# A filter's transform taken about time 0, with tables of its own

## The chip, the cores and the metric

The kernel runs on one core of one Trainium2 chip. The metric is the device time of one execution in microseconds; runs are compared with runs of the same state (fast), on the same chip and in the same rounds. One execution of each kernel is profiled; all times "at" some point are from the start of that profile's span. The engines are PE (matmul), PEld (its weight loads), DVE (vector), ACT (scalar), POOL (GpSimd) and SP. Tiles named ps_... lie in PSUM, which the matmuls here write to; the other tiles lie in SBUF. To evict is to copy a result out of PSUM; a gather is a load whose rows are picked by a tile of indices.

## The reference, cut to what matters

Linear attention with a normalised output, then a long convolution in the frequency domain between two gates, for a batch of 8, 576 time steps and 512 channels:

```python
kv = np.einsum('bhsd,bhse->bhde', k, v)                    # per head, 64 x 64
out = np.einsum('bhsd,bhde->bhse', q, kv)
x = out / sqrt(mean(out * out) + 1e-6) * g_norm            # -> [8, 576, 512]
x1, x2, x3 = split(x @ w_proj, 3)
H = np.fft.rfft(filter_fft, n=576, axis=0)                 # the filter: once for all batches
x2_conv = np.fft.irfft(np.fft.rfft(x2, axis=1) * H, axis=1)
return (x1 * x2_conv * x3) @ w_out
```

The transforms are matmuls with tables of cosines and sines. The change concerns `H`, which is computed once, in the start of the kernel, and is needed before batch 0 can be multiplied by it.

## The kernel before

The start, in the order of the program: loads of the first q, k and v, of three parts of `w_proj` (wp), of the filter (fa and its mirror image fc), of batch 1 and of `w_out`, all issued by POOL; attention of batch 0; transposed tables (FW, FX); then for batch 0 the projection x2, the sums and differences of the filter (ff), the gates (ps_x), the transform of the filter (`gen_h`, tiles ps_h), attention of batch 1 (qT, kvblk), and the first product of a transformed x2 with the filter (tile tpw). From there on DVE is full until about 60 us, and then PE to the end.

The base tables are symmetric about the time 287.5, so the filter was folded about that time too: row n with row 575 - n.

```python
for a, r0, n, base in ((0, 0, 64, 0), (0, 64, 64, 1), (1, 0, 64, 2), (1, 64, 64, SB), (2, 0, 32, SB + 1)):
    nc.gpsimd.iota(fidx[r0:r0 + n, a:a + 1], ..., base=S - 1 - base, channel_multiplier=-3)
for r0, n, a, na, base, step in (...):                     # fa: three direct loads of 64, 64 and 32 rows
    nc.gpsimd.dma_start(out=fa[r0:r0 + n, a:a + na], in_=...)
for a in range(3):                                         # fc: gathers of 128, 128 and 32 rows
    n = P if a < 2 else 32
    nc.gpsimd.indirect_dma_start(out=fc[:n, a], in_=moe_filter_fft, in_offset=...fidx[:n, a:a + 1]...)
# ... cut
def fold_filter():                                         # ff = fa + fc and fa - fc, on DVE, four pieces
    ...
def gen_h(g):                                              # g = 0, 1, 2
    ...                                                    # 6 (or 12) matmuls of FW with ff into hp
    for i, (o_, ri, c1, c2) in enumerate(todo):            # a rotation by the phase of 287.5
        nc.scalar.activation(out=u[:n, i], in_=hp[:n, ri], func=AF.Copy, scale=c1)
        nc.vector.scalar_tensor_tensor(out=o_, in0=hp[:n, 1 - ri], scalar=c2, in1=u[:n, i], ...)
    if g < 2:
        nc.scalar.activation(out=HH[:n, g, 2], in_=HH[:n, g, 0], func=AF.Copy, scale=-1.0)
```

P is 128, S 576, SB 192, N1 97, DM 512 (a row of the filter is 2 KB).

## Time and profile before

| | kernel before |
|---|---|
| time, median | 242.26 us (3 runs, 242.19 to 243.76) |
| span of the profiled run | 238.0 us |
| granted PE clock, mean | 0.993 |
| first filter product (tpw) | 44.56 us |
| from there to the end of the span | 193.4 us |

The span is the profiled core's from its first to its last instruction. The last row is the one to keep: if a change touches only the start, a kernel's span should be its own first tpw plus some 193 us. Two lines of the page of before, in 40 slices of 5.95 us, are for later comparison: the granted clock of PE in tenths, and the busy share of the 16 DMA engines.

```profile
PEclk9999999999999999999999999999999999999997
DMA  6999999999099129914992399250033003400346
```

The clock is at its full value up to the last slice, and the transfers are dense for the first ten slices.

### The profile page before, as it was taken

What the parts mean: (1) busy time and instruction counts of PE and PEld (TensorE: products, weight loads), DVE (VectorE), ACT (ScalarE), POOL (GpSimd) and SP (SyncE); (2) the same over time, 40 slices, a digit from 0 to 9 for tenths busy, and PEclk for the clock granted to TensorE, in tenths of its full rate; (3) what the DMA queues carried; (4) which work ended last, traced back from release to release, by engine and by line L of the source; (5) the groups of instructions that cost most, each with busy time, mean ns of one, the idle gap of its engine ahead of it and who ended that gap; (6) DMA issues with size and microseconds to landing.
All of it is one profiled execution on the core that took longest, in us unless ns stands there. A gap on an engine that the chain in (4) does not pass through costs nothing.

```text
span 238.0 us, 4900 instructions
## 1 busy us (share of the span) xinstructions
PE 213.9 (90%) x1960; PEld 128.5 (54%) x1960; DVE 197.2 (83%) x376; ACT 156.0 (66%) x237; POOL 72.1 (30%) x96
## 2 busy tenths in 40 slices
PE   4978897685999999999999999999999999999960
PEld 1434354363576657665667566656675666566420
DVE  7759574799989798979797989797979897999860
ACT  2754528971887689776977697769776977642520
POOL 7963971490280029000910091002100210021010
PEclk9999999999999999999999999999999999999997
DMA  6999999999099129914992399250033003400346
GB/s 63 163 190 230 227 192 197 191 192 108 3 155 198 45 77 158 203 38 126 121 193 74 91 118 188 83 135 0 4 88 88 3 0 91 132 0 3 94 122 181
DMA packets 45559, 27.17 MB, mean 114 GB/s; under 512 B 22274, under 2 KB 40706, under 8 KB 45538
## 3 DMA queue, kind: packets, MB, share of 16 engines
q0 software_dynamic: 40256, 17.70, 58.8%
q1 hardware_dynamic: 5122, 8.92, 13.9%
q8 instruction: 15, 0.25, 0.4%
q10 hardware_dynamic: 160, 0.26, 0.4%
q14 instruction: 6, 0.05, 0.1%
HBM read 33.69 MB, written 9.44 MB: 181 GB/s over the span
## 4 chain that ended last, share of the span: by engine, by line
PE 61%; ACT 15%; DVE 8%; DMA 8%; issue 3%; POOL 3%; POOLq 0%; DVEq 0%; ACTq 0%
PE ps_x L428 20%; PE ps_out L488 10%; ACT qT L256 6%; PE ps_x L378 6%; DMA fc<-in_moe_filter_fft_dram,fidx 5%; DMA km<-in_k_dram 3%; PE ps_x L384 2%; PE ps_x L369 2%; PE ps_o L265 2%; PE ps_r L280 2%; ACT kvblk L234 2%; PE ps_invo L454 2%; PE ps_inve L454 2%; PE ps_kv L223 2%; ACT osb L271 2%
## 5 line engine op out<-in xcount | busy, mean ns | idle before, releaser
L428 PE MATMUL ps_x<-x,wp 128*128 128x288 bf16 x512 | 68.0, 286 | 1.5 <-DVE FX L210 1.5
L428 PEld LDWEIGHTS <-wp 128*128 128x128 bf16 x512 | 49.8, 98 | 15.3 <-issue 2.6
L411 POOL TENSOR_TENSOR Y<-tpw 128x1024 bf16<-128x1024 f32 (+1 forms) x9 | 21.2, 2354 | 68.7 <-PE ps_x L428 43.2
L434 DVE TENSOR_TENSOR g<-ps_x,x 128x576 bf16<-128x576 f32 x32 | 24.1, 754 | 9.8 <-ACT x L432 9.7
L432 ACT CAST x<-ps_x 128x576 bf16<-128x576 f32 x32 | 20.7, 646 | 10.4 <-PE ps_x L428 10.4
L70 POOL DMA_DIRECT2D km<-in_k_dram x9 | 7.8, 871 | 64.4 <-PE ps_kv L223 64.4
L488 PE MATMUL ps_out<-wo,yg 128*128 128x512 bf16 x112 | 26.6, 379 | 0.0
L281 ACT ACTIVATE rstd<-ps_r,bias_eps 128x576 bf16<-128x576 f32 x32 | 23.3, 742 | 4.8 <-PE ps_r L280 4.8
L496 ACT COPY ot<-ps_out 128x1024 f32<-128x1024 f32 (+1 forms) x17 | 15.9, 937 | 13.8 <-PE ps_out L488 13.8
L266 ACT ACTIVATE sq<-ps_o 128x576 bf16<-128x576 f32 x32 | 20.7, 653 | 5.6 <-PE ps_o L265 5.6
L408 DVE TENSOR_TENSOR tpw<-ps_X,HH 128x1024 f32<-128x1024 f32 (+1 forms) x16 | 19.5, 1221 | 5.1 <-PE ps_X L406 4.4
L271 ACT ACTIVATE osb<-ps_o,g_col 128x576 bf16<-128x576 f32 x28 | 20.8, 742 | 0.0
L409 DVE TENSOR_TENSOR tpw<-ps_X,HH 128x1024 f32<-128x1024 f32 (+1 forms) x16 | 19.4, 1213 | 0.0
L458 ACT COPY os<-ps_invo 128x576 f32<-128x576 f32 x14 | 9.0, 640 | 12.9 <-PE ps_x L372 5.1
L488 PEld LDWEIGHTS <-yg 128*128 128x128 bf16 x112 | 10.8, 98 | 10.4
L265 PE MATMUL ps_o<-qT,kvblk 128*128 128x288 bf16 x64 | 12.8, 287 | 3.7 <-ACT kvblk L234 2.1
L378 PE MATMUL ps_x<-wp,ab 128*128 128x512 bf16 x64 | 15.5, 381 | 0.6 <-DVE ab L307 0.3
L256 ACT COPY qT<-ps_qT 128x1152 bf16<-128x1152 bf16 x14 | 15.1, 1122 | 0.1
L280 PE MATMUL ps_r<-sq,ind 128*128 128x288 bf16 x64 | 13.1, 286 | 1.6 <-ACT osb L271 0.8
L79 POOL DMA_DIRECT2D qb<-in_q_dram x16 | 12.5, 784 | 6.3 <-DMA wp<-in_moe_w_proj_dram 3.1
L535 PE MATMUL ps_w<-kvblk,ind 128*128 128x512 bf16 x33 | 11.1, 486 | 3.7 <-DVE ind L103 3.4
L374 ACT CAST x<-ps_x 128x1024 bf16<-128x1024 f32 x8 | 8.1, 1016 | 8.4 <-PE ps_x L372 8.4
(177 smaller groups left out, 414.8 us busy)
## 6 DMA issues: line engine op xcount, KB each, us to landing
out_dram<-ot SPq DMA_DIRECT2D x28, 256.0 KB, 3.3
qb<-in_q_dram POOLq DMA_DIRECT2D x16, 288.0 KB, 7.1
km<-in_k_dram POOLq DMA_DIRECT2D x7, 512.0 KB, 6.2
vm<-in_v_dram POOLq DMA_DIRECT2D x7, 512.0 KB, 8.4
wp<-in_moe_w_proj_dram POOLq DMA_DIRECT2D x3, 512.0 KB, 10.6
out_dram<-ot SPq DMA_DIRECT2D x10, 128.0 KB, 3.2
km<-in_k_dram POOLq DMA_DIRECT2D x2, 256.0 KB, 5.6
kt<-in_k_dram POOLq DMA_DIRECT2D x8, 64.0 KB, 5.7
```

What stands on the lines that cost most here:

```text
L256: nc.scalar.copy(out=o_, in_=i_)
L266: nc.scalar.activation(out=s['sq'][:, j].rearrange("p (a b) -> p a b", a=2), in_=op[:, :, 0:TH], func=AF.Square)
L271: nc.scalar.activation(out=o_, in_=op[:, :, 0:TH], func=AF.Copy, scale=g_col)
L281: nc.scalar.activation(out=s['rstd'][:, j].rearrange("p (a b) -> p a b", a=2), in_=r2[:, :, 0:TH], func=AF.Abs_reciprocal_sqrt, scale=1.0 ...
L378: nc.tensor.matmul(pp[:, h], ab[:, j, h * SB:h * SB + P], wp[:, j, DM:2 * DM], start=(j == 0), stop=(j == NDC - 1))
L408: nc.vector.tensor_mul(out=t_[:n, 0], in0=xp[:n], in1=HH[:n, g, 1:3])
L409: nc.vector.tensor_mul(out=t_[:n, 1], in0=xp[:n], in1=HH[:n, g, 0:2])
L411: nc.gpsimd.tensor_add(out=Y[:n, 2 * g:2 * g + 2], in0=t_[:n, :, 0], in1=t_[:n, :, 1])
L428: nc.tensor.matmul(pp[:, h, 0:TH], w_, x[:, j, h * TH:(h + 1) * TH], start=(j == 0), stop=(j == NDC - 1))
L432: nc.scalar.copy(out=x1, in_=pp[:, :, 0:TH])
L434: nc.vector.tensor_mul(out=st[b]['g13'][:, dc].rearrange("p (a b) -> p a b", a=2), in0=pp[:, :, 0:TH], in1=x1)
L488: nc.tensor.matmul(pp[:, cc], yg[:, dc, c * P:(c + 1) * P], wo[:, dc], start=(dc == 0), stop=(dc == NDC - 1))
```

## The change

The intent: a filter folded about time 0 (row t with row 576 - t) has a transform that needs no rotation by a phase, so each group of outputs is evicted by one scaled copy instead of ACT and DVE products in turn. It needs tables of its own (FH), which are computed on ACT in an idle gap of 5 us; the base tables shrink from 288 to 192 columns. The filter is now held as 97 partitions of three consecutive rows each. The core of the diff:

```diff
@@ the loads @@
-    for a, r0, n, base in ((0, 0, 64, 0), (0, 64, 64, 1), (1, 0, 64, 2), (1, 64, 64, SB), (2, 0, 32, SB + 1)):
-        nc.gpsimd.iota(fidx[r0:r0 + n, a:a + 1], pattern=[[0, 1]], base=S - 1 - base, channel_multiplier=-3)
-    for r0, n, a, na, base, step in ((0, 64, 0, 2, 0, 2), (64, 64, 0, 2, 1, SB - 1), (0, 32, 2, 1, SB + 1, 1)):
-        nc.gpsimd.dma_start(out=fa[r0:r0 + n, a:a + na], in_=bass.AP( ... ap=[[3 * DM, n], [step * DM, na], [1, DM]]))
+    nc.gpsimd.iota(fidx, pattern=[[-1, 3]], base=S, channel_multiplier=-3)
+    nc.gpsimd.memset(fidx[0:1, 0:1], 0)
+    nc.gpsimd.dma_start(out=fa[:N1], in_=bass.AP( ... ap=[[3 * DM, N1], [1, 3 * DM]]))
     for a in range(3):
-        n = P if a < 2 else 32
-        nc.gpsimd.indirect_dma_start(out=fc[:n, a], out_offset=None, in_=moe_filter_fft,
-                                     in_offset=bass.IndirectOffsetOnAxis(ap=fidx[:n, a:a + 1], axis=0))
+        nc.gpsimd.indirect_dma_start(out=fc[:N1, a], out_offset=None, in_=moe_filter_fft,
+                                     in_offset=bass.IndirectOffsetOnAxis(ap=fidx[:N1, a:a + 1], axis=0))
@@ new tables @@
+    def filter_angles():                    # DVE: 3 products of 289 columns, 3 passes over 97x867
+    def filter_tables():
+        preload_act_table_set("trig_and_small")
+        keep(nc.scalar.activation(out=a_, in_=r_, func=AF.Abs))
+        keep(nc.scalar.activation(out=FH[:N1, :, 1], in_=r_, func=AF.Sin, scale=2 * W0))
+        keep(nc.scalar.activation(out=FH[:N1, :, 0], in_=a_, func=AF.Sin, scale=-2 * W0, bias=cosb[:N1, 0:1]))
+        rsqrt_set()
@@ fold_filter @@
-            for r, c in ((slice(0, P), slice(0, 2)), (slice(0, 32), slice(2, 3))):
-                tc.keep_in_program_order(op(out=ff[r, i, c], in0=fa[r, c], in1=fc[r, c]))
+            tc.keep_in_program_order(op(out=ff[:N1, i], in0=fa[:N1], in1=fc[:N1]))
@@ gen_h @@
-        for i, (o_, ri, c1, c2) in enumerate(todo):
-            nc.scalar.activation(out=u[:n, i], in_=hp[:n, ri], func=AF.Copy, scale=c1)
-            nc.vector.scalar_tensor_tensor(out=o_, in0=hp[:n, 1 - ri], scalar=c2, in1=u[:n, i], op0=ALU.mult, op1=ALU.add)
-        if g < 2:
-            nc.scalar.activation(out=HH[:n, g, 2], in_=HH[:n, g, 0], func=AF.Copy, scale=-1.0)
+        if g == 2:
+            nc.scalar.activation(out=HM, in_=hp, func=AF.Copy, scale=2.0 / S)
+            return
+        nc.scalar.activation(out=HH[:n, g, 0:2], in_=hp[:n], func=AF.Copy, scale=asc[:n] if g == 0 else 2.0 / S)
+        nc.vector.tensor_scalar_mul(out=HH[:n, g, 2], in0=HH[:n, g, 0], scalar1=-1.0)
```

Cut: the smaller `tables()`, the index and angle tiles, and the order of `qtr(1)` and `gen_h(2)`, which change places.

More of the change, by code (lines that the diff above doesn't have):

```diff
@@ L116 @@
     nc.gpsimd.iota(ki[64:128, 2:3], pattern=[[0, 1]], base=2 + 3 * 32, channel_multiplier=3)
-    tvi = work.tile([P, 2 * SB], I32, name="tvi", tag="yg", bufs=3)
-    nc.gpsimd.iota(tvi, pattern=[[2 * SB, 2], [2, 3], [6, 64]], base=1, channel_multiplier=0)
+    tvi = work.tile([P, SB], I32, name="tvi", tag="yg", bufs=3)
+    nc.gpsimd.iota(tvi, pattern=[[2, 3], [6, 64]], base=1, channel_multiplier=0)
+    NF = N1 + SB
+    kri = work.tile([P, NF], I32, name="kri", tag="yg", bufs=3)
+    nc.gpsimd.iota(kri[:, 0:N1], pattern=[[3, N1]], base=0, channel_multiplier=0)
+    nc.gpsimd.iota(kri[:, N1:NF], pattern=[[1, 2], [3, SB // 2]], base=1, channel_multiplier=0)
+    tci = consts.tile([P, 3], I32)
+    nc.gpsimd.iota(tci, pattern=[[1, 3]], base=0, channel_multiplier=3)
     ident = consts.tile([P, P], BF16)
@@ L138 @@
     fidx = consts.tile([P, 3], I32)
-    for a, r0, n, base in ((0, 0, 64, 0), (0, 64, 64, 1), (1, 0, 64, 2), (1, 64, 64, SB), (2, 0, 32, SB + 1)):
-        nc.gpsimd.iota(fidx[r0:r0 + n, a:a + 1], pattern=[[0, 1]], base=S - 1 - base, channel_multiplier=-3)
-    for r0, n, a, na, base, step in ((0, 64, 0, 2, 0, 2), (64, 64, 0, 2, 1, SB - 1), (0, 32, 2, 1, SB + 1, 1)):
-        nc.gpsimd.dma_start(out=fa[r0:r0 + n, a:a + na], in_=bass.AP(
-            tensor=moe_filter_fft.tensor, offset=moe_filter_fft.offset + base * DM,
-            ap=[[3 * DM, n], [step * DM, na], [1, DM]]))
+    nc.gpsimd.iota(fidx, pattern=[[-1, 3]], base=S, channel_multiplier=-3)
+    nc.gpsimd.memset(fidx[0:1, 0:1], 0)
+    nc.gpsimd.dma_start(out=fa[:N1], in_=bass.AP(
+        tensor=moe_filter_fft.tensor, offset=moe_filter_fft.offset, ap=[[3 * DM, N1], [1, 3 * DM]]))
     for a in range(3):
-        n = P if a < 2 else 32
-        nc.gpsimd.indirect_dma_start(out=fc[:n, a], out_offset=None, in_=moe_filter_fft,
-                                     in_offset=bass.IndirectOffsetOnAxis(ap=fidx[:n, a:a + 1], axis=0))
+        nc.gpsimd.indirect_dma_start(out=fc[:N1, a], out_offset=None, in_=moe_filter_fft,
+                                     in_offset=bass.IndirectOffsetOnAxis(ap=fidx[:N1, a:a + 1], axis=0))
     load_q(1)
@@ L155 @@
     nc.vector.tensor_copy(out=kcol, in_=ki)
-    tv = work.tile([P, TH], FP32, name="tv", tag="yg", bufs=3)
-    nc.vector.tensor_copy(out=tv, in_=tvi[:, 0:TH])
-    IV = consts.tile([P, 6, TH], BF16)
-    asc = consts.tile([P, 3], FP32)
-    cf = consts.tile([P, 3, 3], FP32)
-    ph = consts.tile([P, 2, 3], FP32)
-    nc.scalar.activation(out=ph[:, 0], in_=kcol, func=AF.Sin, scale=-W0, bias=cosb[:, 0:1])
-    nc.scalar.activation(out=ph[:, 1], in_=kcol, func=AF.Sin, scale=W0)
+    tv = work.tile([P, SB], FP32, name="tv", tag="ot", bufs=3)
+    nc.vector.tensor_copy(out=tv, in_=tvi)
+    IV = consts.tile([P, 6, SB], BF16)
+    asc = consts.tile([P, 1], FP32)
+    nc.vector.memset(asc, 2.0 / S)
+    nc.vector.memset(asc[0:1], 1.0 / S)
+    nc.vector.memset(asc[96:97], 1.0 / S)
     for c, tag in enumerate(("x", "Y", "g13")):
-        ang = work.tile([P, 2, TH], FP32, name="ang", tag=tag, bufs=1 if c else 2)
+        ang = work.tile([P, 2, SB], FP32, name="ang", tag=tag, bufs=1 if c else 2)
         a_, r_ = ang[:, 0], ang[:, 1]
@@ L176 @@
         nc.scalar.activation(out=IV[:, 2 * c], in_=a_, func=AF.Sin, scale=cosb[:, 2 + h:3 + h], bias=cosb[:, h:h + 1])
-    tc.keep_in_program_order(nc.scalar.preload_act_table_set("abs_reciprocal_sqrt_and_small"))
+    rsqrt_set = lambda: tc.keep_in_program_order(nc.scalar.preload_act_table_set("abs_reciprocal_sqrt_and_small"))
+    rsqrt_set()
+    FH = consts.tile([P, 3, 2, NF], BF16)
+    kr = consts.tile([P, NF], FP32)
+    tcol = consts.tile([P, 3], FP32)
+    fang = {}
+    def filter_angles():
+        nc.vector.tensor_copy(out=kr, in_=kri)
+        nc.vector.tensor_copy(out=tcol, in_=tci)
+        a_, r_ = (work.tile([P, 3, NF], FP32, name="fang", tag="ot", bufs=3)[:N1] for _ in range(2))
+        for a in range(3):
+            nc.vector.tensor_scalar_mul(out=a_[:, a], in0=kr[:N1], scalar1=tcol[:N1, a:a + 1])
+        nc.vector.tensor_scalar(out=r_, in0=a_, scalar1=1.0 / S, scalar2=MAGIC, op0=ALU.mult, op1=ALU.add)
+        nc.vector.tensor_scalar(out=r_, in0=r_, scalar1=MAGIC, scalar2=-1.0 * S, op0=ALU.subtract, op1=ALU.mult)
+        nc.vector.tensor_tensor(out=r_, in0=r_, in1=a_, op=ALU.add)
+        fang['ar'] = a_, r_
+    def filter_tables():
+        a_, r_ = fang['ar']
+        tc.keep_in_program_order(nc.scalar.preload_act_table_set("trig_and_small"))
+        keep = tc.keep_in_program_order
+        keep(nc.scalar.activation(out=a_, in_=r_, func=AF.Abs))
+        keep(nc.scalar.activation(out=FH[:N1, :, 1], in_=r_, func=AF.Sin, scale=2 * W0))
+        keep(nc.scalar.activation(out=FH[:N1, :, 0], in_=a_, func=AF.Sin, scale=-2 * W0, bias=cosb[:N1, 0:1]))
+        rsqrt_set()
+        for p in (0, 96):
+            nc.vector.tensor_scalar_mul(out=FH[p:p + 1, 0, 0], in0=FH[p:p + 1, 0, 0], scalar1=0.5)
     g_col = consts.tile([P, 1], FP32)
@@ L181 @@
         tensor=g_norm.tensor, offset=g_norm.offset, ap=[[0, 2], [1, D]]))
-    FW = consts.tile([P, 3, 6, P], BF16)
+    FW = consts.tile([P, 2, 6, P], BF16)
     FX = consts.tile([P, 4, P], BF16)
@@ L188, in tables @@
         nc.vector.memset(FX[0:96, 0], 0.0)
-        fts = [psp.tile([P, 2, 8, P], BF16, name="ps_ft", tag="ps") for _ in range(2)]
+        d0, d1 = (psp.tile([P, 2, 8, P], BF16, name="ps_ft", tag="ps")[:, 0] for _ in range(2))
         lo, hi = slice(0, 64), slice(64, P)
-        tr = nc.tensor.transpose
-        for a in range(3):
-            n = P if a < 2 else 32
-            ts = slice(a * P, a * P + n)
-            d = fts[a // 2][:n, a % 2]
-            for i in range(6):
-                tr(d[:, i], IV[:, i, ts], ident)
-            if a == 0:
-                tr(d[96:P, 6], IV[:, 1, 0:32], ident)
-                for i in (lo, hi):
-                    tr(d[i, 7], IV[:, 1, 32:96], ident)
-            if a == 1:
-                for i in (3, 5):
-                    tr(d[hi, 6 + i // 5], IV[:, i, P:SB], ident)
-            nc.vector.tensor_copy(out=FW[:n, a], in_=d[:, 0:6])
-            if a == 0:
-                nc.vector.tensor_copy(out=FX[96:P, 0], in_=d[96:P, 6])
-                nc.vector.tensor_copy(out=FX[:, 1], in_=d[:, 7])
-            if a == 1:
-                nc.vector.tensor_copy(out=FX[hi, 2:4], in_=d[hi, 6:8])
+        tr, cp = nc.tensor.transpose, nc.vector.tensor_copy
+        for i in range(2, 6):
+            tr(d0[:, i], IV[:, i, 0:P], ident)
+        tr(d0[0:96, 0], IV[:, 0, 0:96], ident)
+        tr(d0[96:P, 6], IV[:, 1, 0:32], ident)
+        for r in (lo, hi):
+            tr(d0[r, 7], IV[:, 1, 32:96], ident)
+        for i in range(2, 6):
+            tr(d1[lo, i], IV[:, i, P:SB], ident)
+        for i in (3, 5):
+            tr(d1[hi, 6 + i // 5], IV[:, i, P:SB], ident)
+        cp(out=FW[:, 0, 2:6], in_=d0[:, 2:6])
+        cp(out=FW[lo, 1, 2:6], in_=d1[lo, 2:6])
+        cp(out=FX[hi, 2:4], in_=d1[hi, 6:8])
+        cp(out=FW[0:96, 0, 0], in_=d0[0:96, 0])
+        cp(out=FX[96:P, 0], in_=d0[96:P, 6])
+        cp(out=FX[:, 1], in_=d0[:, 7])
     x_t, st = {}, {}
@@ L317, in fold_filter @@
         for i, op in enumerate((nc.vector.tensor_add, nc.vector.tensor_sub)):
-            for r, c in ((slice(0, P), slice(0, 2)), (slice(0, 32), slice(2, 3))):
-                tc.keep_in_program_order(op(out=ff[r, i, c], in0=fa[r, c], in1=fc[r, c]))
-        nc.vector.memset(asc, 2.0 / S)
-        nc.vector.memset(asc[0:1, 0:1], 1.0 / S)
-        nc.vector.memset(asc[96:97, 0:1], 1.0 / S)
-        for i in range(2):
-            nc.vector.tensor_mul(out=cf[:, i], in0=ph[:, i], in1=asc)
-        nc.vector.tensor_scalar_mul(out=cf[:, 2], in0=cf[:, 1], scalar1=-1.0)
-        pc = hst['pc'] = consts.tile([P, 4], FP32, name="pc")
-        for r, o in ((slice(0, 64), (0, 1, 2, 0)), (slice(64, P), (2, 0, 0, 1))):
-            for i in range(4):
-                nc.gpsimd.tensor_copy(out=pc[r, i:i + 1], in_=cf[r, o[i], 2:3])
+            tc.keep_in_program_order(op(out=ff[:N1, i], in0=fa[:N1], in1=fc[:N1]))
     def gen_h(g):
@@ L336, in gen_h @@
         n = N1 if g == 0 else P
-        for ri in range(2):
+        f0 = (0, N1, N1 + P)[g]
+        for i in range(2):
             for a in range(3):
-                m = P if a < 2 else 32
+                m = N1 if a == 0 else N1 - 1
                 kw = dict(start=(a == 0), stop=(a == 2))
                 if g < 2:
-                    nc.tensor.matmul(hp[:n, ri], FW[:m, a, 2 * g + ri, 0:n], ff[:m, ri, a], **kw)
+                    nc.tensor.matmul(hp[:n, i], FH[:m, a, 1 - i, f0:f0 + n], ff[:m, 1 - i, a], **kw)
                 else:
-                    for dup in range(2):
-                        nc.tensor.matmul(hp[dup * NM:(dup + 1) * NM, ri], FW[:m, a, 4 + ri, ri * NM:(ri + 1) * NM], ff[:m, ri, a], **kw)
-        u = work.tile([P, 2, DM], FP32, name="hu", tag="ot", bufs=3)
-        if g < 2:
-            todo = [(HH[:n, g, 1], 0, cf[:n, 0, g:g + 1], cf[:n, 1, g:g + 1]),
-                    (HH[:n, g, 0], 1, cf[:n, 0, g:g + 1], cf[:n, 2, g:g + 1])]
-        else:
-            pc = hst['pc']
-            todo = [(HM[:, i], 0, pc[:, 2 * i:2 * i + 1], pc[:, 2 * i + 1:2 * i + 2]) for i in range(2)]
-        for i, (o_, ri, c1, c2) in enumerate(todo):
-            nc.scalar.activation(out=u[:n, i], in_=hp[:n, ri], func=AF.Copy, scale=c1)
-            nc.vector.scalar_tensor_tensor(out=o_, in0=hp[:n, 1 - ri], scalar=c2, in1=u[:n, i], op0=ALU.mult, op1=ALU.add)
-        if g < 2:
-            nc.scalar.activation(out=HH[:n, g, 2], in_=HH[:n, g, 0], func=AF.Copy, scale=-1.0)
+                    for h in range(2):
+                        cs = (h + i) % 2
+                        nc.tensor.matmul(hp[h * NM:(h + 1) * NM, i], FH[:m, a, cs, f0:f0 + NM], ff[:m, cs, a], **kw)
+        if g == 2:
[3 more added lines that the diff above has]
+        nc.vector.tensor_scalar_mul(out=HH[:n, g, 2], in0=HH[:n, g, 0], scalar1=-1.0)
     def proj2(b):
@@ L539 @@
     qtr(0)
+    filter_angles()
     warm(9)
@@ L550 @@
         fold(0, jj)
+    filter_tables()
     tables()
@@ L562 @@
             gen_h(0)
+            gen_h(2)
             qtr(1)
-            gen_h(2)
             kv(1)
```

## The prediction

> **What bounds the kernel now.** I first read the busy time by stretch, to see where an engine is full, then the chain of work that ended last, then the instructions in order of time for the start, because the change touches only the start (the tables, the filter and its transform; the work on batches 1 to 7 is unchanged, and so are its instructions). Columns of the first view: busy us and count of each engine, clock, DMA share, GB/s.
>
> ```profile
> core 0: us, PE busy (x) PEld busy (x) DVE busy (x) ACT busy (x) POOL busy (x), PEclk, DMA share, GB/s
> 20.00:28.00 8.00, 7.43 (x55) 3.49 (x55) 5.08 (x14) 2.78 (x5) 4.54 (x7) 1.00 1.21 241
> 28.00:36.00 8.00, 6.49 (x40) 3.52 (x38) 6.38 (x9) 2.40 (x4) 6.05 (x15) 1.00 1.57 192
> 36.00:44.50 8.50, 5.86 (x99) 2.92 (x97) 3.83 (x6) 7.49 (x13) 3.20 (x4) 1.00 1.49 195
> 44.50:60.00 15.50, 11.00 (x83) 6.93 (x83) 15.48 (x26) 8.51 (x15) 6.80 (x5) 1.00 1.30 153
> 60.00:84.00 24.00, 23.70 (x232) 15.30 (x233) 21.64 (x39) 18.47 (x28) 6.95 (x7) 1.00 0.76 105
> ```
>
> From 60 us on PE is full, and from 44.5 to 60 DVE is (15.48 of 15.5 us). Before 44.5 nothing is full but the transfers: that stretch is made of waits, and a gain has to come from it. The chain there:
>
> ```profile
> 7.84 6.48 DMA km<-in_k_dram
> 14.36 0.84 issue
> 15.20 0.49 POOL fc L147
> 15.69 0.86 issue
> 16.55 11.37 DMA fc<-in_moe_filter_fft_dram,fidx
> 28.17 1.02 issue
> 29.19 0.55 DVE FW L205
> 29.75 0.31 DVE FX L210
> 30.10 3.10 PE ps_x L428 x24
> 33.20 3.43 PE ps_h L342 x12
> 36.66 1.26 ACT hu L355 x2
> 37.92 1.01 ACT qT L256
> ...
> 42.26 0.76 DVE HM L356
> 43.10 0.70 ACT hu L355
> 43.95 0.61 issue
> 44.56 1.21 DVE tpw L408
> ```
>
> The gathered mirror of the filter (fc) is awaited until about 28. DVE takes its instructions in order, so the copies of the FW and FX tables, which need no fc, wait behind the sum ff; PE waits for their PSUM buffer; then comes the transform (ps_h), and its eviction as an ACT product followed by a DVE product, six times, ping-pong. The first filter product (tpw, 44.56) starts the DVE-bound stage, and whatever moves that instruction should move the end by as much. The start of the wait, in order of time:
>
> ```profile
> 26.02 1.01 ACT L374 CAST x<-ps_x 128x1024 bf16<-128x1024 f32 x1 [5.22 <-PE ps_x L372]
> 28.05 1.23 DVE L319 TENSOR_TENSOR ff<-fa,fc 128x1024 bf16<-128x1024 f32 x1 [2.82 <-DMA fc<-in_moe_filter_fft_dram,fidx]
> ```
>
> ACT is idle for 5.22 us before 26.02: the new tables will be computed in just that gap.
>
> **What the Trainium skill says.** "ScalarE: Activation LUTs", What ACT_TABLE_LOAD costs: a load is about 1283 ns and a switch of sets about 2.66 us with its drain; an activation costs 186 ns plus 0.833 ns an element, a pointer operand 93 ns more. The trace agrees on the load (1283 ns, twice) and on activations (427 ns at 288 columns, 612 with two pointers); in neither case did work stand ready behind the load, so it does not show the drain. "DMA: Bandwidth & Descriptors", Why a DMA increments its semaphore by 16 and not by 1: the largest k up to 16 that divides the slowest dimension is the number of DMA engines a transfer is spread on, so 127 partitions get one; but some direct copies issued by GpSimd were measured to use all, with the partitions divided by 16 and rounded up. Here every transfer of this queue has 128, 64 or 32 rows; the new ones have 97, a prime, and no trace here shows such a one. "VectorE: DVE Perf Modes", The perf-mode tier table: fp32 in SBUF runs at twice the rate for one source, at the plain rate for two; 321 to 358 ns for L170 and L171 against 450 for L172 at 288 columns fits that.
>
> **The change part by part.** I follow the new order of instructions and its semaphores.
>
> *Front.* The base tables have 192 columns for 288, so 12 DVE and 9 ACT instructions are each some 0.1 us shorter, ahead of the first q (landed 9.5): hidden. Added on DVE: kr 0.31, three products of 289 columns at 0.46, two one-source passes of 867 columns and a sum. From L170, L171 and L172 at 288 columns plus 579 more at 0.52 or 1.04 ns: 0.66, 0.62 and 1.05. One pass falls between the two kvblk copies, on the path of batch 0: the front moves back by about 0.6. The last rstd ends at 21.4 for 20.8.
>
> *ACT gap.* Two table loads at 1.28, Abs 0.91, Sin 0.91, Sin with a pointer 1.0, less 0.09 twice for overlap: 5.2. ACT is free at 21.4 + 5.2 = 26.6 to 26.7 for 26.02: the x2 evictions come 0.7 later, the third ends at about 29.1.
>
> *DVE.* The halving of two rows (2 x 0.2) waits for the last Sin (25.4); then four small copies at 0.2 to 0.3 end at 26.8. These release the two PSUM buffers before ff, no longer behind fc (before: 30.05). PE runs the four gate groups, 1.03 each as before, from 26.8 as buffers come free: last from 29.8 to 30.9 (before 33.2).
>
> *Filter.* The bytes are nearly the same, 291 rows for 288 on each side. Landing of fc was 28.3 for the last piece (19.0 + 9.3). With 97 rows over 16 engines the fullest has 7 x 6 KB and 3 x 7 x 2 KB, 84 KB against 72; at 17 GB/s an engine (270 over 16, the rate of 22 to 26 us) up to 0.6 later, partly repaid by longer runs: 28.5. ff is two sums of 97x1536: 1.22 us at 1024 columns plus 512 at 1.04 ns, 1.75 each, 3.4 with overlap (before 4.5 with the table copies in between): ready at 32.0. The transform has the same 24 matmuls, 3.58 + 1.84 us: 32.0 to 37.4 (before it began at 33.04).
>
> *Eviction.* Removed: 6 ACT products at 0.69, 2 at 0.66, 6 DVE products at 0.75, 8 small POOL copies: 5.5 us of ACT and 4.5 of DVE. Added: 3 ACT evictions of 1024 columns at 1.02 and 2 DVE negations at 0.4. On ACT after the last matmul: 1.05 + 2 x 1.07 (qT) + 0.75 (kvblk) ends at 41.4; att_o and the first transform of batch 0 take 1.2 (42.81 to 44.0 before): tpw at 42.6 for 44.56. k and v of batch 1 landed at 36.6, ahead of need at 38.7.
>
> **Sum:** 44.56 - 42.6 = 2.0 us earlier, of which 1.0 is the earlier start of the transform and 1.0 the shorter eviction. The DVE stage is unchanged, so 242.26 - 2.0 = 240.3.
>
> **The rivals.** *Gather on one engine.* If each fc transfer of 97 rows runs on one engine, 97 x 2 KB at about 0.097 us a row (2 KB at 270/16 GB/s, engines 0.8 busy) is 9.4 us after 25.5: lands at 34.9, ff ready 38.4, tpw at 49.0, total about 246.7. The prime row count and the skill's rule speak for it; against it, the exception for direct copies, and that a tuned change would hardly have kept it. If the direct copy fa is hit as well, 291 such units are 28 us after 22.3: lands at 50, total about 262. *Drain.* If each switch costs 2.66, ACT is free 2.8 later, the fourth gate group ends at 33.5 and hides the gain at the transform: 241.8. *Hidden anyway.* If the DVE stage or a load of a later batch sets the pace, the 2 us are lost: 242.3; against it, DVE has no idle time from 44.5 on and no DMA stands in the chain after 28. *More gain.* If fc lands at 27, ff no longer bounds, the gates do (30.9): 239.2.
>
> **Range and chances.** The sum or slightly more gain about 6 in 10, the drain or a lost gain 2 in 10, one engine 2 in 10 (split between 246.7 and 262). So I say 240.3, with 238.4 to 246.0; faster by over 2% (below 237.4) 0.04, slower (above 247.1) 0.12, the rest 0.84.
>
> **What would show it right or wrong.** Right: three ACT instructions between the loads, first x2 eviction at about 26.7; ff right after fc near 28.5; first ps_h about 32; tpw near 42.6 with no DVE idle after it. Wrong: landing of fc or fa well past 30, with a low DMA share while it is awaited; a gap of over 1 us on ACT after a table load; idle DVE between 43 and 58; or kvblk late by more than 1 us in the front.

## The result, and the profile after

| | before | after |
|---|---|---|
| time, median | 242.22 us (4 runs, 240.46 to 243.76) | 249.25 us (4 runs, 248.97 to 250.16) |
| span of the profiled run | 238.0 us | 246.9 us |
| granted PE clock, mean | 0.993 | 0.969 |
| first tpw | 44.56 us | 53.74 us |
| from there to the end | 193.4 us | 193.2 us |

The ratio is 1.0299, with a 95% interval of 1.0223 to 1.0375. Ratios here and below are the mean time of one kernel's fast runs over that of the other's of the same rounds, so not quite the ratio of the medians quoted. The change made the kernel slower; the result is correct.

All of the loss lies ahead of the first tpw: it comes 9.2 us later, and the rest takes the same 193 us. The chain of waits of after, in order of time, answers to the one of before in the prediction (start, us, what):

```profile
13.13 2.40 POOL fc L151
15.83 2.17 POOL fc L151
18.30 20.14 DMA fc<-in_moe_filter_fft_dram,fidx
...
40.23 1.76 DVE ff L348
42.04 5.27 PE ps_h L362 x12
47.31 1.44 PE ps_h L366 x12
```

Three things stand out. The gather of fc, which took 11.37 us on the chain of before, takes 20.14 and ends at 38.44. POOL spends 2.1 to 2.4 us on issuing each gather, for 0.97 to 1.05 before. And the first 12 transform matmuls take 5.27 us, for 3.43 before. The two lines of the page again, in slices of 6.2 us:

```profile
PEclk9999995688999999999999999999999999999998
DMA  6999999999909913992399139931033003400246
```

The DMA line does not show the trouble: its first ten slices are full, as before, because other loads fill the engines. It takes the packets. The trace gives each packet's start, duration and size. Those of the gathers carry two rows, 4096 bytes, and an odd row 2048, which in these two runs tells them from all other traffic of that time. "Busy engines" is the sum of their durations in a stretch over its length:

```
gather packets           after                g112
4096 / 2048 bytes        144 / 3              144 / 48
8 bytes, same queue      2160                 0
per gather               48 pairs + 1 row     16 x (3 pairs + 1 row)
first begins, last ends  24.88, 37.82         22.84, 29.24
busy engines, by 2 us    24: 1.3  26: 3.1     22: 1.2  24: 9.7
(4096 bytes only)        28: 3.1  30: 3.1     26: 8.7  28: 0.8
                         32: 3.1  34: 3.1
                         36: 1.6
median of 4096 bytes     0.241 us             0.262 us
```

(g112 is an experiment below, with 112 rows for 97.) In after, three engines are busy with the gathers for some 12 us. The counts, 48 pairs and a single row three times, fit one gather on each. The packets of 8 bytes, which before and g112 do not have, say the same: 2160 is 15 for each of the 144 pairs, as if each pair went to one engine and the other 15 got a packet without a row.

As to the clock: in the seventh to the tenth slice (37 to 62 us) it falls to 5 to 8 tenths. By stretch (busy us and count of each engine, granted clock, DMA share, GB/s):

```profile
28.00:36.00 8.00, 4.40 (x36) 3.05 (x32) 0.00 (x0) 2.59 (x4) 0.00 (x0) 1.00 1.48 193
36.00:40.00 4.00, 0.00 (x0) 0.00 (x0) 1.44 (x1) 0.00 (x0) 2.21 (x3) 0.61 0.68 76
40.00:44.00 4.00, 1.96 (x5) 0.74 (x6) 3.32 (x4) 0.00 (x0) 1.69 (x3) 0.50 1.25 166
44.00:48.00 4.00, 4.00 (x16) 1.69 (x16) 0.43 (x1) 1.67 (x2) 2.17 (x3) 0.61 1.54 192
```

PE has nothing to do from 32.4 to 42.0, and the clock it is then granted is 0.50 to 0.61: the first 12 matmuls of the transform, which follow the wait, run at about half speed.

What the prediction had been least sure of, the table switch on ACT, went well (start, us, engine, line, operation):

```profile
21.48 1.28 ACT L202 ACT_TABLE_LOAD   x1
22.77 0.93 ACT L204 ACTIVATE fang<-fang 97x867 f32<-97x867 f32 x1
...
25.44 1.28 ACT L180 ACT_TABLE_LOAD   x1
26.89 1.01 ACT L387 CAST x<-ps_x 128x1024 bf16<-128x1024 f32 x1 [0.17 <-PE ps_x L385]
```

The activation behind the first load stood ready, and began 0.01 us after the load's 1.28 us were over. There is no drain to be seen, and the three activations fit into the gap.

### The profile page after: what moved, and what is told of

Its sections match the earlier page's. It is cut to its first block, busy times and chain, and to the rows that moved or that the text cites. A ratio compares the mean times of both kernels' runs of the same rounds, so it can differ in the third digit from the quotient of the medians.

```text
span 246.9 us, 4864 instructions
## 1 busy us (share of the span) xinstructions
PE 214.1 (87%) x1951; PEld 129.3 (52%) x1951; DVE 195.4 (79%) x377; ACT 159.0 (64%) x235; POOL 73.6 (30%) x86
## 4 chain that ended last, share of the span: by engine, by line
PE 59%; ACT 13%; DMA 10%; DVE 8%; POOL 4%; issue 3%; POOLq 0%; DVEq 0%
PE ps_x L441 18%; PE ps_out L501 10%; DMA fc<-in_moe_filter_fft_dram,fidx 8%; ACT qT L286 6%; PE ps_x L391 5%; PE ps_x L397 2%; PE ps_x L382 2%; DMA vt<-in_v_dram 2%; PE ps_o L295 2%; PE ps_h L362 2%; ACT kvblk L264 2%; POOL fc L151 2%; PE ps_r L310 2%; PE ps_invo L467 2%; PE ps_inve L467 2%
## 5 line engine op out<-in xcount | busy, mean ns | idle before, releaser
L501 PEld LDWEIGHTS <-yg 128*128 128x128 bf16 x112 | 10.8, 98 | 10.4
L362 PE MATMUL ps_h<-ff,FH 96*128 96x512 bf16 (+3 forms) x12 | 5.3, 630 | 9.6 <-DVE ff L348 9.6
L548 PE MATMUL ps_w<-kvblk,ind 128*128 128x512 bf16 x33 | 9.5, 429 | 3.7 <-DVE ind L103 3.4
```

Source lines behind the costliest of these rows:

```text
L501: nc.tensor.matmul(pp[:, cc], yg[:, dc, c * P:(c + 1) * P], wo[:, dc], start=(dc == 0), stop=(dc == NDC - 1))
```

## The experiments

My theory: each gather of 97 rows is carried by a single DMA engine because 97 is prime; the late fc costs some 8.5 us directly, and the idle PE loses its clock, which costs the rest. Rivals: the gathers are late for another reason (their place behind other loads, the direct load fa of 97 rows, POOL); and the slow transform has another cause than the clock. Twelve runs were made, on four chips (on which one the result was taken is not recorded); all were correct. The record's verdicts ask for 2%: the change itself is "slower" in both its runs, g112, g112_again and best are "same", and the others that ran more than once "unclear". So the small gains below rest on the intervals of the ratios and on times inside the profiles. Two of the medians include one run in the slow state (g112_again 242.16 us, best 242.96); the ratios leave it out.

### Gathers of 112 rows (g112)

```diff
-        nc.gpsimd.indirect_dma_start(out=fc[:N1, a], ... ap=fidx[:N1, a:a + 1] ...)
+        nc.gpsimd.indirect_dma_start(out=fc[:112, a], ... ap=fidx[:112, a:a + 1] ...)
```

The 15 further rows are valid rows of the filter that nothing reads. 112 is 16 x 7.

> The changed kernel, with one edit: each of the three gathers of the mirrored filter takes 112 rows (15 of them unused) instead of 97. Theory 1 (a gather of 97 rows, a prime, is put on one DMA engine, so three engines carry all of it): the last gather lands near 28.5 to 29.5 us instead of 38.4, a POOL issue of it takes about 1.0 us instead of 2.2, the DMA share does not fall to two or three tenths, and the time is about 240.3 us, ratio 0.99 to the kernel before. Theory 2 (the loss comes from the new tables: the front, the two table loads, the later halving): nothing of that is touched, the time stays near 249 us.

Measured: 238.71 us (13 runs, 238.12 to 239.83) beside 240.79 of the kernel before, ratio 0.9921 (0.9897 to 0.9945). The issue of the gathers, and the chain:

```profile
13.08 1.62 POOL L151 DMA_INDIRECT fc<-in_moe_filter_fft_dram,fidx  x1 [0.23 <-issue]
15.01 1.04 POOL L151 DMA_INDIRECT fc<-in_moe_filter_fft_dram,fidx  x1 [0.30 <-issue]
16.35 0.92 POOL L151 DMA_INDIRECT fc<-in_moe_filter_fft_dram,fidx  x1 [0.30 <-issue]
```

```profile
16.35 13.60 DMA fc<-in_moe_filter_fft_dram,fidx
...
33.56 2.78 PE ps_h L362 x12
36.34 1.44 PE ps_h L366 x12
```

More bytes land sooner: at 29.95 for 38.44. The issue is back to about 1 us for two of the three gathers, the transform runs at full speed, and the first tpw comes at 42.76. So the row count of three gathers is the whole loss, and without it the change is worth 0.8%, the predicted 240.3 over 242.26 being 0.992 as well (which is in part luck, see below). A second run of the same kernel on another chip (below, g112_again) gave 0.990.

### Gathers of 100 rows (g100)

The same edit with 100 for 112.

> The changed kernel with gathers of 100 rows. If the number of DMA engines is the largest divisor up to 16 of the row count, 100 rows run on 10 engines: landing 1 to 3 us after that of 112 rows, near 30 to 32, and a POOL issue slightly over 1 us. If rows are spread by rounding up (7 each on 15 engines), it lands as 112 rows do. If only 97 as the true row count were at fault for another reason (say the rows wanted), it lands as before, near 38. Time 240 to 243 in the first two.

Measured: one run, 239.67 us (state unknown, as for every kernel run only once); ff begins at 31.86, for 30.07 with 112 rows and 38.56 with 97:

```profile
L348 DVE TENSOR_TENSOR ff<-fa,fc x2: 1749/1754/1758, 31.9 to 33.5; 97x1536 bf16<-97x1536 f32 x2
```

So it is no matter of a multiple of 16. The 100 rows land 1.8 us later than 112, and about 7 us earlier than 97; the packets are 150 pairs, as ten engines with five pairs each of three gathers would have them, and 90 of 8 bytes, as the six other engines would have in each of these 15 steps.

### A prime number above 97 (g103)

The same edit with 103.

> The changed kernel with gathers of 103 rows, again a prime, six more than 97. Theory (the largest divisor up to 16 decides the engines): one engine for each gather again, fc landing 103/97 later than the 12 to 14 us of 97 rows, so at 39 to 42; tpw 54 to 57, total about 250. Rival (something of 97 itself, or of rows just over 96): fc lands near 30 as with 100 and 112 rows, total about 240.

Measured: one run, 251.92 us; fc lands at 39.94, 1.0 us later than with 97 rows on the same chip (38.94), and the first tpw comes at about 56.6:

```profile
18.98 20.96 DMA fc<-in_moe_filter_fft_dram,fidx
```

Its packets are 153 pairs and 3 single rows, three times 103 rows, on 3.1 busy engines again, with 2295 packets of 8 bytes, again 15 for each pair. Six rows more at 0.12 us (half of the 0.241 us of a pair) make 0.7 of the 1.0 us; its first packet also began 0.7 later, so this sum is rough. But three rows more than 100, and 8 us later: the divisors decide, as the theory says.

### The kernel before, with its gathers cut at row 97 (b_split97)

```diff
-        n = P if a < 2 else 32
-        nc.gpsimd.indirect_dma_start(out=fc[:n, a], ... ap=fidx[:n, a:a + 1] ...)
+        for r0, r1 in ((0, N1), (N1, P)) if a < 2 else ((0, 32),):
+            ix = fidx2 if r0 else fidx
+            nc.gpsimd.indirect_dma_start(out=fc[r0:r1, a], ... ap=ix[0:r1 - r0, a:a + 1] ...)
```

The rest of the rows has an index tile of its own (fidx2), which two instructions on POOL fill.

> The kernel before, with each of its two gathers of 128 rows cut into one of 97 and one of 31 (both primes), the same rows and bytes, results unchanged. Theory 1: the slow landing moves into the kernel before: last landing near 37 to 39 us instead of 28.3, POOL issue of the 97-row ones about 2.2 us, and the time about 8 us longer, near 250. Theory 2 (the gather is not to blame): landing near 28 to 29 and 242 to 243 us.

Measured: 248.14 us (4 runs, 247.87 to 249.17), ratio 1.0326 (1.0245 to 1.0408). The same bytes go to the same places:

```profile
22.28 13.61 DMA fc<-in_moe_filter_fft_dram,fidx
...
38.97 4.77 PE ps_h L346 x9
```

The two gathers of 97 rows take 2.24 and 2.14 us to issue, those of 31 (a prime too) 1.34 and 1.35. The last landing is at 35.89, the transform slow again, the first tpw at 51.71. Part of the lateness is that five gathers are issued for three, the last until 24.93 for 20.03; but the rows of fc go on until 35.5 us, with 3.7 busy engines from 28 to 30 us and 1.2 from 34 to 36, so here too few engines carry them. This puts a loss like that of the change into the old kernel with nothing of its tables, its ACT work or its load of fa: these rivals are out.

### Useless matmuls in PE's wait (a_warm, a_warm2)

```diff
+        if g == 1:
+            for _ in range(44):             # a_warm2: 54
+                tc.keep_in_program_order(nc.tensor.matmul(
+                    hp[:, 0], ind, kvblk[1].rearrange("p a b -> p (a b)"), start=True, stop=True))
```

> The changed kernel, gathers of 97 rows kept, with 44 matmuls of no use (into the PSUM tile that the transform then overwrites) in TensorE's wait for the gather. They test what of the loss is the clock, which fell to 0.5 to 0.6 after TensorE stood idle from 32.4 to 42.0. If the clock costs: the first twelve matmuls of the transform take about 3.6 us instead of 5.27, the first filter product starts 1.0 to 2.0 us earlier, and the time is 247 to 248. If it costs nothing because others set the pace: within 0.5 us of 249.3. Landing of the gather unchanged near 38.4 in both.

Measured: 251.43 us (4 runs, 250.62 to 253.23), ratio 1.0438 (1.0358 to 1.0518), slower rather than faster, and no answer. In that profile fc landed at 40.89, 2.4 us later than in the profile of after; the useless matmuls ended 2.0 us before ff was ready, and the first 12 matmuls of the transform still took 4.44 us. (It lost besides in the way that the run best shows below: x took 5.04 us.) So the expectation was missed, and two questions remained: does PE's work delay the gather, and does the clock explain the slow transform? The second try has ten matmuls more, and runs beside the unaltered change on one chip.

> The changed kernel unaltered, as a control on the chip of the next three runs. Expected: ratio to before about 1.03, fc landing at 38 to 41, the first 12 transform matmuls at about half speed (5.3 us for 2.8), first tpw 53.7 (or later by as much as fc lands later, if the chip of the run with 44 useless matmuls was simply another).

> The changed kernel with 54 useless matmuls in PE's wait for ff, ten more than the first try, so that they end at about 44.5 and not 2 us before ff is ready. Theory (the idle wait lowers the granted clock, which stretches the transform): the first 12 transform matmuls take about 2.8 us for 5.3, and from the first transform matmul to the first tpw pass 9.2 us (the run with gathers of 112 rows) for 11.7. Rival (the stretch is longer for another reason, such as transfers in the way): 11.7 us or so stays. The total may be longer, since the useless matmuls run past the readiness of ff if fc lands early; only the stretch counts.

Measured: after_again 250.42 us (4 runs, 249.04 to 250.96), ratio 1.0417 (1.0372 to 1.0462), so the loss is there on a second chip and somewhat larger. Its ff begins at 39.06, that of a_warm2 at 38.81: the useless matmuls do not delay the gather, and the later landing of the first try was that run's own. Its pairs of rows took 0.273 us in the median for 0.241 in after, and the first began 0.8 us later; why is open. (The issue is not the reason: the first gather took 2.75 us to issue there, and 2.83 in a_warm2.) The matmuls of the transform in after_again, ns as least/median/most:

```profile
L362 PE MATMUL ps_h<-ff,FH x12: 377/634/634, 42.5 to 46.8; 96*128 96x512 bf16 x4, 96*97 96x512 bf16 x4, 97*128 97x512 bf16 x2, 97*97 97x512 bf16 x2
```

and in a_warm2:

```profile
L366 PE MATMUL ps_h<-ff,FH x12: 377/379/381, 44.6 to 47.0; 96*128 96x512 bf16 x4, 96*97 96x512 bf16 x4, 97*128 97x512 bf16 x2, 97*97 97x512 bf16 x2
```

With PE kept busy all 12 take 377 to 381 ns. From the first transform matmul to the first tpw pass 9.2 us (44.61 to 53.80) for 11.3 (42.55 to 53.83): the clock cost 2.1 us in that run, and in the profile of after 11.7 less the 9.2 of g112, 2.5 us. (The total of a_warm2, 251.81 us in its one run, gains nothing: the useless matmuls run until 44.6, past the 42.5 at which ff was ready, and the first tpw comes where it came before.)

### Two evictions moved from ACT to DVE (best)

The row count being settled, I looked for what could be had on top. In g112 DVE is idle for 4.81 us before the first tpw, while ACT works through HM (the last part of the filter's transform), two copies of qT and kvblk, one after another.

```diff
-            nc.scalar.activation(out=HM, in_=hp, func=AF.Copy, scale=2.0 / S)
+            nc.vector.tensor_scalar_mul(out=HM, in0=hp, scalar1=2.0 / S)
@@ qtr @@
-            if b == 0:
+            if b == 0 or (b == 1 and jj == 1):
                 tc.keep_in_program_order(nc.vector.tensor_copy(out=o_, in_=i_))
```

> The changed kernel with gathers of 112 rows, and two evictions of the start moved from ACT to DVE, which is idle for 4.81 us before the first tpw there: HM (1.02 us on ACT) and the second half of qT (1.07). On ACT the chain from the transform to kvblk gets about 1.4 to 2 us shorter, bounded by the matmuls of kv (end 39.5). Expected: first tpw at 41.0 to 41.4 for 42.76, ratio to before about 0.986 (0.992 with 112 rows alone). If the DVE stage does not begin with tpw but has slack behind it, 0.992 stays.

Measured: 240.15 us (20 runs, 238.76 to 242.96), ratio 0.9961 (0.9937 to 0.9985). This is less than g112 gained. The front of the profiled run was 2 us late, and still the first tpw came at 42.38; but from there to the end it took 196.3 us for 193.3. Most of the missing 3 us lies in one instruction (DVE and POOL behind the first tpw):

```profile
45.96 2.36 POOL L424 TENSOR_TENSOR Y<-tpw 128x1024 bf16<-128x1024 f32 x1
46.92 5.05 DVE L319 TENSOR_TENSOR x<-osb,rstd 128x1152 bf16<-128x1152 bf16 x1
...
48.97 2.37 POOL L424 TENSOR_TENSOR Y<-tpw 97x1024 bf16<-97x1024 f32 x1
```

The product x takes 0.76 us elsewhere, and 5.05 here; it ends 0.6 us after the second of POOL's sums. In g112 it came later with respect to the first sum and slipped through between the two, and only d_, the second DVE instruction after it, was held:

```profile
47.29 0.96 DVE L319 TENSOR_TENSOR x<-osb,rstd 128x1152 bf16<-128x1152 bf16 x1
48.17 0.74 DVE L447 TENSOR_TENSOR g<-ps_x,x 128x576 bf16<-128x576 f32 x1
48.28 2.37 POOL L424 TENSOR_TENSOR Y<-tpw 97x1024 bf16<-97x1024 f32 x1
48.84 2.23 DVE L329 TENSOR_TENSOR d__656<-x 128x768 bf16<-128x768 bf16 x1
```

In all, 4.3 us were lost to POOL in best for 1.9 in g112, so 2.4 of the 3; the rest is open. The product g, with one input in PSUM, keeps its 0.74 us. This is what the Trainium skill says, in "SBUF — State Buffer", Who interferes with whom: a DVE instruction with two inputs in SBUF contends with a GpSimd instruction that reads SBUF, and whichever comes second stands still until the other has finished. The trace agrees; that x should be held through the gap of 0.65 us between the two sums as well the page does not say.

### The same with one of the two sums on DVE (best2), and a control (g112_again)

```diff
-            if g or not b:
+            if g:
                 nc.gpsimd.tensor_add(out=Y[:n, 2 * g:2 * g + 2], in0=t_[:n, :, 0], in1=t_[:n, :, 1])
@@ batch 0 @@
-            fft(0, 0)
+            add0 = fft(0, 0)
             att_r(1, 1); att_x(1, 0); fold(1, 0)
+            add0()
```

> The changed kernel with gathers of 112 rows once more, as a control on the chip of the next two runs, and to see whether its gain holds on a second chip. Expected: ratio to before 0.992, first tpw near 42.8.

> The changed kernel with gathers of 112 rows and the two evictions moved to DVE, as in the last run, and besides the second filter sum Y of batch 0 on DVE for POOL. In the last run a bf16 product on DVE (x) took 5.05 us for 0.74, from 46.92 to 51.97, while POOL worked on its two Y sums (to 51.34); with 112 rows alone the two products concerned took 0.96 and 2.23. Theory (such a product of DVE stands still while POOL's sum runs, and the earlier tpw moved it into both sums): with one POOL sum only, x takes at most about 2.5 us and d_ its plain 0.54; DVE pays about 1.1 us for the sum itself; the ratio to before comes to about 0.985, less than the 0.992 of 112 rows alone. Rival (the moved evictions cost by themselves, or the later front of the last run, kvblk 2 us later, comes with the kernel): the ratio stays at 0.996, and the front is 2 us late again.

Measured: g112_again 238.88 us (4 runs, 238.44 to 242.16), ratio 0.9899 (0.9802 to 0.9996); best2 237.77 us (4 runs, 237.46 to 238.46), ratio 0.9862 (0.9786 to 0.9938). In best2, x takes 2.00 us and d_ 0.55, and the sum on DVE 1.21:

```profile
46.66 2.00 DVE L319 TENSOR_TENSOR x<-osb,rstd 128x1152 bf16<-128x1152 bf16 x1
```

The first tpw at 42.12 plus 193.7 us makes the span of 235.8. So the 5.05 us came from the two POOL sums, and the late front of the last run was not the kernel's (kvblk at 13.07 here, 13.17 in the control). Between g112 and best2 lie 0.37%, less than their intervals; the profiles, 1.5 us apart at the first tpw on one chip, carry the verdict.

### The order on DVE in the kernel before (b_order)

```diff
+        cp = lambda **kw: tc.keep_in_program_order(nc.vector.tensor_copy(**kw))
-            nc.vector.tensor_copy(out=FW[:n, a], in_=d[:, 0:6])
+            cp(out=FW[:n, a], in_=d[:, 0:6])
```

and likewise for the three FX copies: in the kernel before the scheduler had put two of these copies behind ff, which waits for fc.

> The kernel before with only the order of DVE changed: the copies of the FW and FX tables are kept ahead of the sum ff, which waits for fc. Theory (part of the step of the transform: in the kernel before, the table copies stand behind the wait for fc in DVE's order and hold PE's PSUM buffers, which delays the gates and with them the transform): the gates end by about 31.6 for 33.2, the transform begins at about 31.8 for 33.2 and the first tpw comes about 1.3 us earlier, ratio 0.994 to 0.996. Rival (the transform waits for ff alone, which is as late as before): ratio 1.000.

Measured: 238.08 us (4 runs, 237.97 to 238.48), ratio 0.9868 (0.9794 to 0.9942), more than expected. The chain and order of time at ff:

```profile
26.87 4.09 PE L429 MATMUL ps_x<-x,wp 128*128 128x288 bf16 x32
28.06 0.64 ACT L433 CAST x<-ps_x 128x576 bf16<-128x576 f32 x1 [0.25 <-PE ps_x L429]
28.78 3.55 DVE L320 TENSOR_TENSOR ff<-fa,fc 128x1024 bf16<-128x1024 f32 x4 [2.37 <-DMA fc<-in_moe_filter_fft_dram,fidx]
30.02 0.64 ACT L433 CAST x<-ps_x 128x576 bf16<-128x576 f32 x1 [1.32 <-PE ps_x L429]
30.80 1.95 PE L343 MATMUL ps_h<-ff,FW 128*128 128x512 bf16 x6
```

The gates run without a break before 31, where before 24 of their 32 matmuls waited until 30.10. The transform begins at 30.80 for 33.04, although ff begins 0.7 us later than in the profile of before, because it needs only the first half of ff to begin. The first tpw comes at 42.84, 1.72 us earlier. So this one line of ordering, in the old kernel, gives what the whole change gives once its row count is mended (42.76), and the half of the predicted gain that was to come from an earlier transform needs no new tables at all. (In g112 that half did not come: its transform began at 33.56, 0.5 us later than in before, and its whole gain is the stretch from there to the first tpw, 9.2 us for 11.5.)

### The two sums of ff in the other order (best3)

```diff
-        for i, op in enumerate((nc.vector.tensor_add, nc.vector.tensor_sub)):
+        for i, op in ((1, nc.vector.tensor_sub), (0, nc.vector.tensor_add)):
```

> The last best version (gathers of 112 rows, two evictions and one filter sum on DVE) with the two sums of ff in the other order. The transform of the changed kernel reads the difference first (it is made last), so PE waits for both sums, 3.43 us after fc lands; the kernel before read the sum first and began 1.25 us ahead of the end of ff in the run with the table copies in order (30.80 for 32.3). Theory: the first three transform matmuls run 1.7 us earlier, the next wait for the sum, and the transform as a whole and the first tpw come about 0.7 us earlier; ratio to before about 0.983 for 0.986. Rival (the gates of batch 0, which end near 32.2, or the loads set the transform): ratio 0.986 as before. A difference of 0.3% lies near what the intervals can resolve; the times inside the profile decide.

Measured: 237.28 us (4 runs, 237.06 to 237.90), ratio 0.9838 (0.9766 to 0.9910); the first three matmuls of the transform run at 32.10, the rest from 33.41 (34.21 in best2), and the first tpw comes at 41.41 for 42.12. But that gain is not the order's: ff began 0.80 us earlier in this profile, which is of another chip (first line best2, then best3):

```profile
30.73 3.43 DVE L348 TENSOR_TENSOR ff<-fa,fc 97x1536 bf16<-97x1536 f32 x2 [2.90 <-DMA fc<-in_moe_filter_fft_dram,fidx]
29.93 3.43 DVE L348 TENSOR_TENSOR ff<-fa,fc 97x1536 bf16<-97x1536 f32 x2 [2.98 <-DMA fc<-in_moe_filter_fft_dram,fidx]
```

Counted from there, the first tpw comes after 11.48 us, for 11.39 in best2. The matmuls behind the transform (qT) do begin 0.65 us sooner, so counted, but the ones after them (kv) then wait for a load of v until 38.6 us: one of the rivals of the expectation, the loads. The version has the lowest ratio of all, 1.6% below the kernel before and so ahead of both kernels; but its interval overlaps with those of best2 and b_order, and the three are not told apart.

## Why the prediction was wrong

I said 240.3 us, and 238.4 to 246.0; it was 249.25 us, slower by 3.0%. Step by step:

- **The step that failed is *Filter*:** "With 97 rows over 16 engines the fullest has 7 x 6 KB and 3 x 7 x 2 KB, 84 KB against 72 ...: 28.5." In its place: each gather of 97 rows behaves as if carried by one engine, and fc lands at 38.4. The rule was on the table, from the Trainium skill ("DMA: Bandwidth & Descriptors", Why a DMA increments its semaphore by 16 and not by 1). I set it aside for its exception, which the page gives for direct copies and not for gathers, and for the thought "that a tuned change would hardly have kept it", which is no evidence at all. The runs show the rule for gathers (97 and 103 slow, 100 between, 112 fast) and agree with the exception for the direct copy: the 97 packets of fa in after, of 6144 bytes each, all lie between 21.97 and 25.26 us, and keep 10.9 engines busy from 22 to 24. (The sum written there for the spread case is slightly off as well: 12 KB more at 17 GB/s are 0.7 us, not 0.6.)
- **The rival that came true, *Gather on one engine*, was mis-sized.** It said landing at 34.9, tpw at 49.0 and a total of 246.7. Its term was 97 rows at 0.097 us from 25.5 on, 9.4 us. The packets of the gathers began at 24.9, and summed to 36.9 us on three engines (all 4096-byte packets of after), 12.3 us for each: 0.127 us a row. The last ended at 37.8, and the semaphore was seen at 38.4. The start was right and the rate was not: I had divided the traffic of all engines by 16 and 0.8, where one engine alone moved 4096 bytes in 0.241 us, pauses not counted.
- **The loss of clock was not foreseen at all,** and is worth 2.1 to 2.5 us (a_warm2 against after_again; after against g112). The Trainium skill has it in "TensorE: Matmul & The Clock Gate", Part 1: after an idle window of about 3.4 us PE falls to half its clock. The traces agree in kind: with PE idle for 9.6 us, the granted clock fell to half at 36.9 us and rose again at 47.1; after the 1.24 us of g112 it was full. A wait of PE is therefore to be counted with what follows it.
- **Sum of the loss,** in profiles: against g112, fc makes ff start 8.5 us later (38.56 and 30.07) and the clock makes the stretch from the transform to tpw 2.5 us longer. Together 11.0; the spans differ by 10.8 (246.9 and 236.1).
- ***Front* was right:** batch 0's first attention matmul came 0.75 us later (14.60 for 13.85; 14.18 in g112, where k and v had landed sooner), predicted 0.6. ***ACT gap* was right:** the first x2 eviction at 26.89, predicted 26.7; the rival *Drain* is out. ***DVE*, the release of the table buffers at 26.8, was nearly right:** the last table copy ends at 27.07; but the gates ran from 28.31 to 32.40, not to 30.9, behind matmuls of x2 that I had not put ahead of them.
- **The predicted gain was right only in its sum.** With the gathers mended, the first tpw comes at 42.76, predicted 42.6. But fc landed at 29.95 and the transform began at 33.56, not at 32.0; and from there to tpw it took 9.2 us, not 10.6. The second error is that of the matmuls: I had taken 5.4 us from the rows of before; they take 4.2. In before the first 12 start 0.31 to 0.34 us apart on each step into or out of the piece of 32 rows, and 0.21 to 0.26 on the others; in g112, where the pieces have 97, 96 and 96 rows, 0.22 on every step. Of the first, half a microsecond may be the 15 further rows (3 x 15 x 2 KB at 200 GB/s); the rest is open. Two errors of 1.5 us cancelled, and the sum proves less than it seems to.
- ***Hidden anyway* is out:** in every profile without the long collision on POOL (a_warm, a_warm2 and best have it) the span is the first tpw plus 193 to 194.4 us, so whatever moves tpw moves the end.

## What to carry to other kernels

Before changing the number of rows of a gather, look at its divisors: 97 for 128 cost 3%, and 15 useless rows more (112) gave it back and 0.8% besides. Size a wait of PE with the slower clock behind it, and watch what a moved instruction will meet on the other engines: an earlier DVE product ran into two POOL sums and lost 4.3 us, where 1.9 had been lost before. And look first for plain order: putting four table copies ahead of a wait in the old kernel gave as much as the whole mended change.

## What the Trainium skill lacked or had wrong

- "DMA: Bandwidth & Descriptors": the rule of the largest divisor is confirmed for gathers, which its examples do not name (fc landing at 38.4 with 97 rows, 39.9 with 103, about 31.8 with 100, 29.95 with 112). It lacks what the small number costs besides: the issue of a gather on POOL took 2.1 to 2.8 us with 97 rows and 0.9 to 1.7 with 112, and the queue carried 15 packets of 8 bytes for every pair of rows (2160 in after, none in g112).
- The same page: no rate of one engine under such a gather; here a packet of two rows (4096 bytes) took 0.241 us in the median, 17 GB/s, and 97 rows 12.3 us.
- "ScalarE: Activation LUTs": its 2.66 us for a switch of table sets with drain did not show. With work ready behind it, the load's 1.28 us was all (the next activation began 0.01 us later in after, 0.02 in g112).
- "SBUF — State Buffer": the lock between DVE and POOL is as it says, but x stood still through a gap of 0.65 us between two POOL sums (5.05 us in all), and in a_warm and a_warm2 again (5.04 and 4.88 us).
- "TensorE: Matmul & The Clock Gate": its half clock after an idle window is confirmed. The page names an idle window of 3.4 us; in a_warm 2.0 us without matmuls before the transform were enough (the first 12 took 4.44 us for 2.78), and 1.24 us in g112 were not. The kept traces show more: within a trace, stretches of half clock start whole multiples of 3.41 us apart. Cut on that grid, every piece of 3.41 us with PE idle for 1.84 us or more was followed by half clock (28 pieces of all 14 traces, from 8 us on), and none with 1.66 or less that began at full clock; in between there are both. So where the pieces fall matters: the gap of some 2 us ahead of the first tpw fell into two pieces in g112 and cost no clock, and into one in g112_again (2.15 us), where half clock was granted from 43.5 to 46.9 us.
